# Twelve weight loads moved from SyncE's DMA queue to ScalarE's, in a pooled-attention and spatial-gating kernel

## The chip, the core and the metric

The kernel runs on one core of a Trainium2 chip. A core has a matrix engine (PE; its weight loads are listed apart as PEld), a vector engine (DVE), a scalar engine (ACT, ScalarE), GpSimd (POOL) and SyncE (SP), which here only starts transfers. Each engine works through its own list of instructions in order, and waits on semaphores where it needs another engine or a transfer (DMA). Transfers started by SP or by ACT are carried by the core's 16 DMA engines.

The metric is the device time of one execution in microseconds. It is read as the median of several executions.

## The reference

For each of 8 batches the reference computes attention with 8 heads of 64 on 576 tokens, where keys and values are averaged over groups of 8 tokens (72 pooled ones), and then a gated layer with weights that all batches share. Cut to what matters:

```python
k_p = k.reshape(B, H, Sp, pool, D).mean(axis=3); v_p = ...      # 576 -> 72
attn = softmax(scale * q @ k_p.T);  x = (attn @ v_p) as [B, S, 512]
h = np.maximum(x @ w_in, 0.0)                # w_in [512, 1024]
u, v = h[..., :512], h[..., 512:]
v_n = (v - mean(v)) / np.sqrt(var(v) + 1e-06)
v_s = np.einsum('ts,bsd->btd', w_spatial, v_n) + b_spatial[None, :, None]
out = (u * v_s) @ w_out                      # w_out [512, 512]
```

The inputs reach the device in double width: two 32-bit words stand for each element of `w_in` and `w_out`, so a block of 128 x 512 weights is a transfer of 512 KB, and the kernel makes of it a high part and a low part (`win_h`, `win_l`, `wout_h`, `wout_l`) in the format of the matrix engine.

## The kernel before, in words

All weights, the keys of a batch and its intermediate tiles live on chip. A stage is a short generator: each piece up to a `yield` is one step. The attention stages of a batch are K and KT (keys: load, pool, transpose), V and W (values), Q0 to Q3 (queries of two heads each), S0 to S3 (scores and softmax), T and Y (transposed probabilities) and A (attention output, tile `xT`). The gated layer's are v (`x @ w_in`, right half, and normalisation), u (left half), s (the product with `w_spatial`) and o (the product with `w_out` and the store). Batch after batch the stages of attention for the next batch run between the matrix products of this one.

The weights are loaded once, during the first batch. `wv0` to `wv3` are the four blocks of the right half of `w_in` (128 rows each, line 191, tile `stw`), `wu0` to `wu3` the four of the left half (128 columns each, line 193, tile `stw`), and `wo0` to `wo3` the four of `w_out` (line 191, tile `st`). Each goes through `load_f64`: its first step starts the transfer; its second has ACT read the block (line 202 makes `x` of the high words, line 205 scales the low words, where it is wanted); then DVE (lines 207 to 221) and POOL (lines 212, 213, 224) put the bits together, ACT or POOL writes the high part (lines 229 or 227), and PE and ACT, or POOL (lines 239, 241), the low part.

The order of every engine's work is written out by hand: the string `FIRST` for the first batch, `STEP` for the middle ones, `LAST` for the last. Each word of a string takes the next step of a stage, and all instructions of that step are appended to their engines' lists in that order. A transfer that is started by SP stands in SP's list; one that is started by another engine stands in that engine's list, at the place of its step. Nothing but the string decides that place. `FIRST` begins

```python
"wo1~ -K^ -K wo1 wo1 wo1 -K wv1 -Q0~^ -K wv1 wo1 -K -Q0 wv1 -K wo1 -K wv3^! wv3 -Q1^ wv1 wv1 -KT~ ..."
```

so the second step of `wv3` follows its first one directly, with no other stage between them.

The tiles `stw` are used once for each block and wait for nobody before they are filled. `st` is taken from a ring of three buffers that keys, values and `w_spatial` use too.

Of the kernel before, what the change touches and what calls it, by code (L numbers as in the profile page):

```python
# [10 lines left out]
U32 = mybir.dt.uint32  # L11
# [71 lines left out]
def f32(ap):  # L83
    return ap.bitcast(F32)
# [3 lines left out]
def pooled_attention_gmlp(ctx: ExitStack, tc: tile.TileContext, q, k, v, w_in, w_sp, b_sp, w_out, out):  # L88
    nc = tc.nc
# [9 lines left out]
    NK = DM // P  # L99
# [65 lines left out]
    def ring(tag, bufs, shape, dt, name, pool=pl):  # L165
        return pool.tile(shape, dt, name=name, tag=tag, bufs=bufs)

    def ps_big():
        return ring("mm", 3, [P, 512], F32, "mm", ps)
# [9 lines left out]
    def load_f64(hi, lo, src, alt, st=None):  # L179

        n = DH
        if st is None:
            st = ring("kv", 3, [P, n, 2], U32, "st")
        if len(src.shape) == 2:  # L190
            nc.sync.dma_start(out=st, in_=src.bitcast(U32).rearrange("p (n w) -> p n w", w=2))
        else:
            nc.sync.dma_start(out=st.rearrange("p (c n) w -> p c (n w)", c=NK), in_=src.bitcast(U32))
        yield
        low, high = st[:, :, 0], st[:, :, 1]
        x = ring("vv", 5, [P, n], F32, "x")

        def as_w(ap):
            return ap if len(src.shape) == 2 else ap.rearrange("p (c n) -> p c n", c=NK)

        xi = x.bitcast(U32)
        nc.scalar.activation(x, high.bitcast(F32), AF.Abs, scale=2.0 ** -112)
        if "~" not in alt:
            scaled = low.bitcast(F32)
            nc.scalar.activation(scaled, low, AF.Copy, scale=2.0 ** -52)
        yield
        nc.vector.tensor_scalar(xi, xi, 3, None, op0=ALU.logical_shift_left)
        if "!" in alt:
            yield

            sign, xw = high.bitcast(I32), x.bitcast(I32)
            nc.gpsimd.tensor_scalar(sign, sign, 0.0, -2.0 ** 31, op0=ALU.is_lt, op1=ALU.mult)
            nc.gpsimd.tensor_tensor(xw, xw, sign, op=ALU.add)
            yield
        else:
            nc.vector.scalar_tensor_tensor(xi, high, 0x80000000, xi, op0=ALU.bitwise_and, op1=ALU.bitwise_or)
        y = ring("ob", 2, [P, n], F32, "y")
        nc.vector.tensor_scalar(y.bitcast(U32), xi, 0xFF800000, None, op0=ALU.bitwise_and)
        z = ring("vv", 5, [P, n], F32R, "z") if "^" in alt else y
        if "~" in alt:  # L220
            nc.vector.scalar_tensor_tensor(z, low, 2.0 ** -52, y, op0=ALU.mult, op1=ALU.mult)
        else:
            yield
            nc.gpsimd.tensor_tensor(z, scaled, y, op=ALU.mult)
        yield
        if "%" in alt:
            nc.gpsimd.tensor_copy(hi, as_w(x))
        else:
            nc.scalar.activation(hi, as_w(x), AF.Copy)
        yield  # L230
        if "^" in alt:
            a = ps_big()
            nc.tensor.matmul(a, lhsT=ident, rhs=x, start=True, stop=False)
            nc.tensor.matmul(a, lhsT=ident_m, rhs=hi, start=False, stop=False)
            nc.tensor.matmul(a, lhsT=ident_p, rhs=z, start=False, stop=True)
            yield
            nc.scalar.activation(lo, as_w(a), AF.Copy)
        else:
            nc.gpsimd.tensor_tensor(as_w(x), as_w(x), f32(hi), op=ALU.subtract)
            yield  # L240
            nc.gpsimd.tensor_tensor(lo, as_w(x), as_w(y), op=ALU.add)
# [3 lines left out]
    def load_w_in(half, c, alt=""):  # L245

        tag, n, i = ("gT", NK, c) if half else (("vn_h", "vn_l")[c // 2], 2, c % 2)
        if tag not in staged:

            staged[tag] = pl.tile([P, n, DH, 2], U32, name="stw", tag=tag)  # L250
        cs = slice(c * P, (c + 1) * P)
        if half:
            return load_f64(win_h[:, c, DH:], win_l[:, c, DH:], w_in[cs, DH:], alt, staged[tag][:, i])
        return load_f64(win_h[:, :, cs], win_l[:, :, cs], w_in[:, cs].rearrange("(c p) n -> p c n", p=P), alt,
                        staged[tag][:, i])

    def load_w_out(c, alt=""):
        return load_f64(wout_h[:, c, :], wout_l[:, c, :], w_out[c * P:(c + 1) * P, :], alt)
# [625 lines left out]
```

## Time and profile before

| | before |
|---|---|
| median of 3 runs (lowest to highest) | 551.75 us (551.69 to 552.06) |
| profiled execution, its own time | 551.63 us |
| span of its profile | 549.8 us |
| PE busy | 534.9 us (97%) |
| DVE, ACT, POOL busy | 340.0, 291.6, 278.4 us (62%, 53%, 51%) |
| DMA engines' mean busy share | 42.0% |
| granted TensorE clock | 1.00 |

The span is what lies between the first and the last recorded event; the remaining 1.83 us of the execution lie around it. The chain that ended last is followed back from the last instruction, at each step to what released it. A row of a timeline gives start, duration, engine, line, operation and tiles, and in brackets how long the engine had been idle before and what ended that. SPq is SP's list: the time in such a row is that of starting a transfer, not that of carrying it.

### The profile page before, as it was taken

The numbers are of one execution on the slowest core, as the hardware profiler recorded it, in microseconds if no ns is written. First come the engines' busy times: TensorE is split into PE (matmuls) and PEld (weight loads), VectorE is DVE, ScalarE is ACT, GpSimd is POOL, SyncE is SP. The second block draws the span as 40 slices with busy tenths as digits, with TensorE's granted clock in tenths as the row PEclk, the third lists the DMA queues.
The fourth block names the chain that finished last, engine by engine and source line by source line (L and its number), as shares of the span: only waits on it lengthen the run. The fifth ranks groups of instructions, "written<-read, shape, count | busy, mean of one in ns | idle before, by whom it ended". The sixth has DMA issues, their size and how long they took to land.

```text
span 549.8 us, 11810 instructions
## 1 busy us (share of the span) xinstructions
PE 534.9 (97%) x4293; PEld 477.8 (87%) x4293; DVE 340.0 (62%) x785; ACT 291.6 (53%) x958; POOL 278.4 (51%) x375
## 2 busy tenths in 40 slices
PE   4799999999999999999999999999999999999997
PEld 4588799988998889988998889988998889989995
DVE  3568989987756377675666477675666576623110
ACT  2598788655545365455465365455465554424321
POOL 3845554951457273574825574574825534303340
PEclk9999999999999999999999999999999999999999
DMA  7877463459314363436616264446615232001102
GB/s 242 248 238 157 109 136 111 111 167 236 72 50 115 85 153 76 124 106 153 160 50 162 74 170 107 121 111 155 157 38 136 97 84 93 13 0 39 38 2 97
DMA packets 123354, 63.11 MB, mean 115 GB/s; under 512 B 84256, under 2 KB 104736, under 8 KB 123296
## 3 DMA queue, kind: packets, MB, share of 16 engines
q1 hardware_dynamic: 123296, 62.35, 42.0%
q8 instruction: 34, 0.56, 0.4%
q14 instruction: 24, 0.20, 0.1%
HBM read 44.92 MB, written 17.40 MB: 113 GB/s over the span
## 4 chain that ended last, share of the span: by engine, by line
PE 89%; POOL 3%; ACT 2%; DMA 2%; issue 1%; DVE 1%; SPq 1%; POOLq 0%; ACTq 0%; DVEq 0%
PE mm L780 19%; PE mm L803 18%; PE mm L761 17%; PE mm L718 16%; PE s_ps L530 4%; PE mm L734 2%; DMA qt<-in_q 2%; PE tp L667 2%; PE tp L670 2%; PE mm L781 2%; PE mm L782 2%; PE tp L669 1%; PE tp L668 1%; PE mm L321 1%; POOL vn_l L728 1%
## 5 line engine op out<-in xcount | busy, mean ns | idle before, releaser
L761 PE MATMUL mm<-xT,win_h 128*128 128x320 f32 (+1 forms) x512 | 103.1, 296 | 0.0
L761 PEld LDWEIGHTS mm<-xT,win_h 128*128 128x128 f32 x512 | 82.2, 188 | 2.4
L794 POOL TENSOR_TENSOR gT<-g,gT 128x256 fp32r<-128x256 f32 x64 | 46.5, 736 | 72.5 <-ACT gT L791 72.4
L803 PE MATMUL mm<-wout_h,gT 128*128 128x512 f32 x256 | 79.8, 393 | 0.0
L718 PE MATMUL mm<-win_h,xT 128*128 128x512 f32 x256 | 79.6, 392 | 0.0
L780 PE MATMUL mm<-wT_h,vn_h 128*128 128x256 f32 (+1 forms) x256 | 77.3, 302 | 0.0
L780 PE MATMUL mm<-wT_h,vn_l 128*128 128x256 f32 (+1 forms) x256 | 75.9, 297 | 0.1
L780 PE MATMUL mm<-wT_l,vn_h 128*128 128x256 f32 (+1 forms) x256 | 75.6, 295 | 0.0
L761 PE MATMUL mm<-xT,win_l 128*128 128x320 f32 (+1 forms) x256 | 75.2, 294 | 0.0
L513 POOL TENSOR_TENSOR e<-e,rs 128x576 f32<-128x576 f32 (+1 forms) x32 | 44.9, 1404 | 52.9 <-DVE rs L511 49.4
L785 DVE TENSOR_TENSOR g<-mm,ru 128x256 f32<-128x256 f32 (+1 forms) x64 | 27.7, 450 | 54.1 <-PE mm L782 52.6
L705 POOL TENSOR_TENSOR rstd<-rstd,neg_half 128x1 f32<-128x1 f32 (+1 forms) x40 | 23.2, 583 | 68.3 <-DVE rstd L703 68.2
L506 ACT ACTIVATE e<-s_ps,mx 128x72 f32<-128x72 f32 x190 | 57.6, 332 | 0.2
L728 POOL TENSOR_TENSOR vn_l<-vv,vn_h 128x512 fp32r<-128x512 f32 x32 | 43.0, 1354 | 28.0 <-ACT vn_h L726 28.0
L803 PEld LDWEIGHTS mm<-wout_h,gT 128*128 128x128 f32 x256 | 47.0, 188 | 9.5
L718 PEld LDWEIGHTS mm<-win_h,xT 128*128 128x128 f32 x256 | 47.1, 188 | 9.4
L791 ACT ACTIVATE gT<-g 128x256 fp32r<-128x256 f32 x64 | 25.8, 413 | 47.0 <-DVE g L785 47.0
L699 DVE BATCH_NORM_STATS2 st<-vv 128x6 f32<-128x512 f32 (+1 forms) x40 | 27.3, 682 | 37.7 <-ACT vv L722 37.6
L803 PE MATMUL mm<-wout_l,gT 128*128 128x512 f32 x128 | 50.5, 395 | 0.0
L718 PE MATMUL mm<-win_l,xT 128*128 128x512 f32 x128 | 50.3, 393 | 0.0
L780 PEld LDWEIGHTS mm<-wT_h,vn_h 128*128 128x128 f32 x256 | 48.2, 188 | 2.0 <-ACT ru L764 0.9
L780 PEld LDWEIGHTS mm<-wT_h,vn_l 128*128 128x128 f32 x256 | 48.3, 189 | 0.8 <-POOL vn_l L728 0.5
(191 smaller groups left out, 1260.4 us busy)
## 6 DMA issues: line engine op xcount, KB each, us to landing
st<-in_k SPq DMA_DIRECT2D x32, 256.0 KB, 4.6
out<-ob SPq DMA_DIRECT2D x32, 256.0 KB, 2.0
qt<-in_q SPq DMA_DIRECT2D x112, 72.0 KB, 3.2
st<-in_v SPq DMA_DIRECT2D x24, 256.0 KB, 4.2
xd<-X SPq DMA_DIRECT2D x24, 256.0 KB, 2.5
pt_l<-xd SPq DMA_DIRECT2D x24, 256.0 KB, 3.7
stw<-in_moe_w_in SPq DMA_DIRECT2D x8, 512.0 KB, 7.0
st<-in_moe_w_out SPq DMA_DIRECT2D x4, 512.0 KB
```

The source lines that it names most:

```text
L506: nc.scalar.activation(em[:, h, :], sv[:, h % 2, h // 2, :], AF.Exp, bias=mx[:, h:h + 1], scale=QK, accum_out=sm[:, h:h + 1])
L513: nc.gpsimd.tensor_tensor(em, em, rs.unsqueeze(2).broadcast_to([P, n, SP]), op=ALU.mult)
L699: nc.vector.bn_stats(st6[:m], vv[:m])
L705: nc.gpsimd.tensor_tensor(rstd[:m], rstd[:m], neg_half[:m], op=ALU.pow)
L718: nc.tensor.matmul(a, lhsT=xT[:, i, o + c * P:o + (c + 1) * P], rhs=w[:, i, DH:], start=(i == 0 and j == 0), stop=(i == NK - 1 and j == 2))
L728: nc.gpsimd.tensor_tensor(t["vn_l"][:, c, :], vv, f32(t["vn_h"][:, c, :]), op=ALU.subtract)
L761: nc.tensor.matmul(a, lhsT=w[:, i, d * P:(d + 1) * P], rhs=xT[:, i, o + ts.start:o + ts.stop], start=(i == 0 and j == 0), stop=(i == NK - ...
L780: nc.tensor.matmul(a, lhsT=x[:, c, ds], rhs=y[:, c, ts], start=(c == 0 and j == 0), stop=False)
L785: nc.vector.tensor_tensor(g, a, t["ru"][:, d, ts], op=ALU.mult)
L791: nc.scalar.activation(dst[:, d, 0, at:at + m], g[:, o:o + m], AF.Copy)
L794: nc.gpsimd.tensor_tensor(dst[:, d, 1, at:at + m], g[:, o:o + m], f32(dst[:, d, 0, at:at + m]), op=ALU.subtract)
L803: nc.tensor.matmul(a, lhsT=src[:, i, x, at:at + m], rhs=w[:, i, :], start=(i == 0 and j == 0), stop=(i == ND - 1 and j == 2))
```

## The change

The two lines of `load_f64` that start the transfer of a weight block name `nc.scalar` instead of `nc.sync`. All twelve transfers are those of before, with the same sizes and tiles, and the strings of the order are untouched.

```diff
         if len(src.shape) == 2:
-            nc.sync.dma_start(out=st, in_=src.bitcast(U32).rearrange("p (n w) -> p n w", w=2))
-        else:
-            nc.sync.dma_start(out=st.rearrange("p (c n) w -> p c (n w)", c=NK), in_=src.bitcast(U32))
+            nc.scalar.dma_start(out=st, in_=src.bitcast(U32).rearrange("p (n w) -> p n w", w=2))
+        else:
+            nc.scalar.dma_start(out=st.rearrange("p (c n) w -> p c (n w)", c=NK), in_=src.bitcast(U32))
         yield
```

The lists of PE, DVE and POOL are the same in both kernels. What moves stands in ACT's and SP's lists. At the start of ACT's list, which holds no transfer before, these are the rows of the change (from the first block, `wo1`, over `wv1` and `wv3` to `wv2`):

```order
L191 DMA st<-in_moe_w_out 128x1024
L202 ACT_TABLE_LOAD
L202 ACTIVATE x<-st 128x512
L229 ACTIVATE wout_h<-x 128x512
L191 DMA stw<-in_moe_w_in 128x1024
L202 ACTIVATE x<-stw 128x512
L205 ACTIVATE stw<-stw 128x512
L362 COPY kp<-mm 128x256
L363 COPY kr<-mm 64x128
L191 DMA stw<-in_moe_w_in 128x1024
L202 ACTIVATE x<-stw 128x512
L205 ACTIVATE stw<-stw 128x512
```

The second and the third transfer (`wv1`, `wv3`) stand directly ahead of the instruction that reads what they bring. In SP's list of before these rows stand at the same stage:

```order
L191 DMA st<-in_moe_w_out 128x1024
L344 DMA st<-in_k 128x1x512 x4
L331 DMA st_r<-in_k 64x1x512
L191 DMA stw<-in_moe_w_in 128x1024
L452 DMA qt<-in_q 128x4x64 x2
L453 DMA qt<-in_q 64x2x64
L191 DMA stw<-in_moe_w_in 128x1024
L452 DMA qt<-in_q 128x4x64 x2
```

Without the three weight rows SP's list begins with the keys, and the queries follow them directly. Further on in ACT's list, still in the first batch, the blocks `wu2` and `wu1` come in between the softmax and the copies of the attention output; these are the rows of the change:

```order
L193 DMA stw<-in_moe_w_in 128x4x256
L638 ACTIVATE pt_rr<-tp 32x64 x2
L506 ACTIVATE e,sm<-s_ps,mx 128x72 x10
L175 ACTIVATE xT<-tp 128x256
L193 DMA stw<-in_moe_w_in 128x4x256
L175 ACTIVATE xT<-tp 128x320 x2
L237 ACTIVATE win_l<-mm 128x512
L202 ACTIVATE x<-stw 128x512
```

Here the first of the two (`wu2`) stands some fifteen instructions ahead of line 202, which reads it.

## The prediction

> **What bounds the kernel now.** I read the page first, for the busy shares and the chain that ended last:
>
> ```profile
> PE 534.9 (97%) x4293; PEld 477.8 (87%) x4293; DVE 340.0 (62%) x785; ACT 291.6 (53%) x958; POOL 278.4 (51%) x375
> PE 89%; POOL 3%; ACT 2%; DMA 2%; issue 1%; DVE 1%; SPq 1%; POOLq 0%; ACTq 0%; DVEq 0%
> ```
>
> PE bounds it. Since the moved transfers all lie in the first batch, the stretches come next (columns: stretch, its length, busy time of PE, PEld, DVE, ACT, POOL, granted clock, DMA share, GB/s):
>
> ```profile
> 0.00:25.00 25.00, 15.23 (x158) 12.62 (x158) 11.69 (x30) 9.01 (x17) 13.60 (x18) 1.00 0.80 240
> 25.00:549.00 524.00, 519.67 (x4136) 465.16 (x4136) 328.35 (x756) 282.57 (x941) 264.83 (x358) 1.00 0.41 109
> ```
>
> From 25 us on PE idles 524.00 - 519.67 = 4.33 us in all. So whatever makes PE late by 25 us goes to the end nearly whole. Ahead of 25 us PE idles 9.8 us, and the chain there runs through other engines (the chain in order of time: start, length, what):
>
> ```profile
> 14.74 0.37 ACT kp L362
> ...
> 15.27 0.56 ACT x L202
> 15.83 0.57 ACT stw L205
> 16.41 0.52 ACT win_h L229
> ...
> 24.87 0.49 PE mm L235
> ```
>
> Between the last two stand POOL and DVE with the same block. The rows "ACT x L202" and "ACT stw L205" are the conversion of block `wv3`. They stand on the chain now, with no gap from line 362 to line 229: nothing on ACT can be added there for free. What ACT did and what it waited for (timeline):
>
> ```profile
> 4.42 0.66 ACT L202 ACTIVATE x<-st 128x512 f32<-128x512 f32 x1 [2.42 <-DMA st<-in_moe_w_out]
> 6.30 0.63 ACT L229 ACTIVATE wout_h<-x 128x512 fp32r<-128x512 f32 x1 [1.22 <-DVE x L216]
> 11.64 0.66 ACT L202 ACTIVATE x<-stw 128x512 f32<-128x512 f32 x1 [4.71 <-DMA stw<-in_moe_w_in]
> 12.21 0.66 ACT L205 ACTIVATE stw<-stw 128x512 f32<-128x512 uint32 x1
> 14.74 0.37 ACT L362 COPY kp<-mm 128x256 f32<-128x256 f32 x1 [1.88 <-PE mm L321]
> 15.17 0.67 ACT L202 ACTIVATE x<-stw 128x512 f32<-128x512 f32 x1
> ```
>
> and when SP started those transfers (timeline):
>
> ```profile
> 0.72 0.40 SPq L191 DMA_DIRECT2D st<-in_moe_w_out  x1
> 1.19 2.62 SPq L344 DMA_DIRECT2D st<-in_k  x4
> 4.62 0.40 SPq L191 DMA_DIRECT2D stw<-in_moe_w_in  x1
> 6.85 0.59 SPq L191 DMA_DIRECT2D stw<-in_moe_w_in  x1
> 15.34 0.53 SPq L393 DMA_DIRECT2D st<-in_v  x1
> ```
>
> `wv3` was started at 6.85 us and was there when ACT came to it at 15.17, 8.3 us later: ACT did not wait for it.
>
> **The price of a block, from start to use.** Before, `wo1` took 4.42 - 0.72 = 3.70 us with nothing ahead of it, `wv1` 11.64 - 4.62 = 7.02 us with keys ahead of it. The value blocks of the same size give 6.7 (transfers: KB each, median us to landing), and two windows of the first batch give the rate that the DMA engines reach when they are full:
>
> ```profile
> st<-in_v SPq DMA_DIRECT2D x4, 512.0 KB, 6.7
> 5.00:10.00 5.00, 3.54 (x16) 3.57 (x17) 2.24 (x4) 0.71 (x2) 2.78 (x2) 1.00 0.94 290
> 20.00:25.00 5.00, 3.78 (x40) 2.64 (x31) 3.08 (x6) 1.81 (x5) 4.38 (x4) 1.00 0.97 307
> ```
>
> Alone, 0.524 MB at 0.29 MB/us are 1.8 us, so of `wo1`'s 3.70 some 1.9 are fixed. In a list of its own a block no longer queues behind SP's transfers, but shares the engines with them: at half of 0.307 MB/us it takes 3.4 us, and 5.3 with the fixed part. I take 5.3 and keep 3.7 and 7.0 as ends. The Trainium skill says why half is likely (page "DMA: Bandwidth & Descriptors", section "Queues, rings and completion order"): SP and ACT own one row of rings each, on the same 16 engines, and an engine goes round between the rows packet by packet. No trace here shows it, since before has one such queue. Were a block served as quickly as `wo1` was, with 3.7 in place of 5.3 in steps 2 and 3, the sum below would be 2.8 + 1.0 = 3.8 us and the time 555.4.
>
> **The change part by part.**
>
> 1. *`wo1`* starts at 0.72 as before, but the keys no longer stand behind it. It lands between 4.42 (as before) and 6.46, when PE got its first keys:
>
> ```profile
> 6.46 1.84 PE L321 MATMUL mm<-st,ident 128*128 128x128 f32 x7 [6.46 <-DMA st<-in_k]
> 12.78 0.66 PE L467 MATMUL tp<-ident,qt 128*128 128x128 f32 x4 [0.51 <-DMA qt<-in_q]
> ```
>
>    I take 5.3, near the early end since its start is as early as that of the first keys. From line 202 to the end of line 229 ACT took 6.30 + 0.63 - 4.42 = 2.51 us, so ACT comes to the next transfer at 7.8 (6.9 to 9.0).
>
> 2. *`wv1`* starts there instead of at 4.62, and ACT sits in the next instruction until it lands: 7.8 + 5.3 = 13.1 (6.9 + 3.7 = 10.6 to 9.0 + 7.0 = 16.0). Lines 202 and 205 take 12.21 + 0.66 - 11.64 = 1.23 us: 14.3 (11.8 to 17.2). The cover is ACT's idle 1.88 us ahead of line 362, where it waits for PE to pool the keys. PE may be there earlier than 14.74: SP starts the keys 1.19 - 0.72 = 0.47 us sooner and PE need not wait 0.51 for the queries, so 13.76 at best. Line 362 then starts at 14.3 (13.8 to 17.2), and line 363 ends 15.27 - 14.74 = 0.53 later: 14.9 (14.3 to 17.8).
>
> 3. *`wv3`* is the step that decides. Its transfer stands behind lines 362 and 363, and its reader directly behind it. It starts at 14.9 and lands at 14.9 + 5.3 = 20.2 (14.3 + 3.7 = 18.0 to 17.8 + 7.0 = 24.8). What shares the engines with it are the value block that SP starts at 15.34, and the ones behind it. Line 202 begins at 20.2 and not at 15.17: 5.0 us late (2.8 to 9.6). Queued behind it on ACT are line 205, line 229 (`win_h`), the copies of `qT` and the exponentials. POOL waits for line 229, DVE stands in line 207 for this `x`, ahead of the last copy of the keys, and PE waits for that copy:
>
> ```profile
> 17.00 1.27 POOL L239 TENSOR_TENSOR x<-x,win_h 128x512 f32<-128x512 f32 x1 [1.61 <-ACT win_h L229]
> 16.19 0.42 DVE L207 TENSOR_SCALAR x<-x 128x512 uint32<-128x512 uint32 x1
> 16.52 0.40 DVE L379 COPY kT<-tp 64x32 f32<-64x32 f32 x2
> 16.75 0.95 PE L530 MATMUL s_ps<-kT,qT 64*64 64x72 f32 x32 [0.15 <-DVE kT L379]
> ```
>
>    All of them move by the same 5.0, and no slack is to be seen: POOL had waited 1.61 us for line 229, PE 0.15 for line 379. Late next is everything behind PE's line 235 at 24.87, from where PE has work without a gap.
>
> 4. *The nine later blocks* cost ACT their starting time, and that of SP falls away. By line (ns, minimum, median, maximum) SP took
>
> ```profile
> L191 SPq DMA_DIRECT2D st<-in_moe_w_out x4: 347/376/442, 0.7 to 88.7; - x4
> L191 SPq DMA_DIRECT2D stw<-in_moe_w_in x4: 399/593/687, 4.6 to 22.6; - x4
> L193 SPq DMA_DIRECT2D stw<-in_moe_w_in x4: 503/588/1186, 21.9 to 44.8; - x4
> ```
>
>    I take the same for ACT. It counts where ACT is on the chain:
>
> ```profile
> 37.21 0.21 ACT pt_rr L638
> 37.67 3.14 ACT e L506 x20
> 82.86 0.67 ACT x L202
> ```
>
>    `wu2` starts directly ahead of line 638 at 37.21 and `wo0` just ahead of line 202 at 82.86: 0.59 + 0.38 = 1.0 us. The others stand ahead of an instruction that waits anyway (`wv2` ahead of line 500, which idled 1.85 us for DVE), or behind one that PE needs: nothing. Ends: nothing at all, if these are hidden too, and 0.59 (`wv0`) + 1.19 + 0.59 (`wu1`) + 0.38 = 2.75, if each is paid and `wu2` at its longest.
>
> ```profile
> 19.34 0.68 ACT L500 ACTIVATE e<-e 128x576 f32<-128x576 f32 x1 [1.85 <-DVE e L498]
> 42.02 0.77 ACT L202 ACTIVATE x<-stw 128x512 f32<-128x512 f32 x1
> ```
>
>    Their landing is covered: from `wu2`'s start to its line 202 there are 42.02 - 37.21 = 4.8 us of ACT's own work and two starting times, 6.0 us against 5.3; at 7.0 us it would cost 1.0.
>
> 5. *SP* loses twelve starts. The 0.47 us at the keys are in step 2; later SP waits for buffers, so I count nothing. The Trainium skill (page "Perfetto Trace Analysis", section "DMA Optimizations") has the rule that spreading transfers over issuing engines may help where an engine's issuing is the bottleneck. SP's rows from 0.72 on are dense, so by that rule there would be a gain; it is the rival below.
>
> Sum: 5.0 + 1.0 = 6.0 us. Against the profiled execution's own time, 551.63 (its span of 549.8 and 1.83 around it; 0.12 below the median 551.75), that is **557.6 us**, 1.1% slower.
>
> **The rivals.**
>
> *All early blocks at their late ends.* `wo1` shares fully with the keys, `wv1` and `wv3` take 7.0 each: 9.6 us at step 3, and 1.0: 562.2. For it: the 7.0 and 6.7 above. Against: those were measured behind a full queue, which ACT's list doesn't have.
>
> *Given back later.* The shift eats the 4.33 us that PE idles after 25 us: 557.6 - 4.3 = 553.3. Against: these gaps are waits for engines that are late themselves.
>
> *SP's freed queue wins: faster.* The keys come 0.47 us sooner, PE's 0.51 for the queries goes, and the early starts ahead of keys and queries (0.40 and 0.59) no longer hold SP up: 0.47 + 0.51 + 0.40 + 0.59 = 1.97 us, 549.7. For it: PE's first work waits for keys at 6.46. It decides only if `wv3` makes line 202 less than 1.97 us late, so if it lands by 17.1; started at 14.3 that is 2.8 us, less than the shortest price of 3.7.
>
> *The change doesn't do what it says.* If ACT started transfers ahead of instructions that still wait, `wv3` would be on its way by 8 us and nothing would change: 551.6. Against: it stands behind line 363 in the list, and no row shows an engine's list out of order.
>
> **How the numbers follow.** My forecast has 0.62, the late ends 0.20, the shift given back 0.08, the faster case 0.05, the unchanged one 0.05. The bounds of the forecast alone are 551.63 + 2.8 = 554.4 and 551.63 + 9.6 + 2.75 + 1.0 = 565.0; the upper one needs all ends at once. With the case given back and most of the late one, the range is 553.0 to 563.5. About 0.2% (1.1 us) is what can be told from no change here: faster 0.05, same 0.05, slower 0.90.
>
> **What would show it.** In the changed profile line 202 should wait for `stw<-in_moe_w_in` twice, the second time some 5 us around 20 us; POOL's line 239 on `win_h` should start at 22 and PE's line 235 near 30. From there to the end the span should be as long as before, within 1 us or so. I am wrong if line 202 for `wv3` does not wait, if PE's line 235 comes at 25 to 27 us, or if the time is lost behind 30 us.

## The result, and the profile after

The changed kernel takes 555.61 us (median of 4 runs, 555.12 to 556.42), the kernel before in the same series 551.72. The ratio is 1.0074, with a 95% interval of 1.0061 to 1.0087: 3.9 us or 0.7% slower. The forecast was 557.6 us. The profiled execution took 555.23 us, 1.83 around a span of 553.4, so it lies 3.6 us above that of before and at the low side of its runs.

The page of the changed kernel, busy shares and the chain that ended last:

```profile
PE 536.4 (97%) x4293; PEld 479.5 (87%) x4293; DVE 340.4 (62%) x785; ACT 291.6 (53%) x958; POOL 278.7 (50%) x375
PE 90%; DMA 3%; ACT 2%; POOL 2%; DVE 1%; issue 1%; SPq 0%; POOLq 0%; ACTq 0%; DVEq 0%
```

ACT's busy time is the same to the tenth (291.6), since starting a transfer is not counted as busy. The page hardly shows the change; DMA on the chain rose from 2% to 3%. The timeline of ACT shows it (rows with ACTq are the starts):

```profile
6.34 0.63 ACT L229 ACTIVATE wout_h<-x 128x512 fp32r<-128x512 f32 x1 [1.22 <-DVE x L216]
8.13 0.34 ACTq L191 DMA_DIRECT2D stw<-in_moe_w_in  x1
12.33 0.67 ACT L202 ACTIVATE x<-stw 128x512 f32<-128x512 f32 x1 [5.36 <-DMA stw<-in_moe_w_in]
12.91 0.67 ACT L205 ACTIVATE stw<-stw 128x512 f32<-128x512 uint32 x1
12.91 0.33 ACTq L191 DMA_DIRECT2D stw<-in_moe_w_in  x1
13.47 0.35 ACT L362 COPY kp<-mm 128x256 f32<-128x256 f32 x1
18.21 0.66 ACT L202 ACTIVATE x<-stw 128x512 f32<-128x512 f32 x1 [4.22 <-DMA stw<-in_moe_w_in]
```

Line 202 now waits for `stw` twice. The first wait, for `wv1`, is 5.36 us instead of 4.71. The second, for `wv3`, is new: 4.22 us, and line 202 begins at 18.21 instead of 15.17, 3.04 us late. The chain of waits runs through both transfers:

```profile
2.76 5.34 DMA st<-in_k
8.13 4.18 DMA stw<-in_moe_w_in
12.33 0.58 ACT x L202
12.91 5.27 DMA stw<-in_moe_w_in
18.21 0.67 ACT x L202
18.90 0.43 DVE x L207
19.33 0.10 DVE kT L379
19.47 1.49 PE s_ps L530 x32
...
58.14 5.51 PE mm L718 x24
...
535.35 13.76 PE mm L803 x60
```

The chain of before has the last two of these rows as well:

```profile
55.15 5.51 PE mm L718 x24
...
532.33 13.76 PE mm L803 x60
```

So the shift is 58.14 - 55.15 = 2.99 us at the first group of line 718 and 535.35 - 532.33 = 3.02 us at the last group of line 803. What was lost by 19 us is carried through 480 us unchanged; on balance nothing is added on the way and nothing given back. The chain puts the second start down to the end of line 202 at 12.91; PE had pooled the keys 0.04 us before that, at 12.87, so this profile alone can't tell which of the two the start followed. Who waited for `wv3` is seen at POOL and PE:

```profile
20.02 1.27 POOL L239 TENSOR_TENSOR x<-x,win_h 128x512 f32<-128x512 f32 x1 [3.95 <-ACT win_h L229]
19.47 1.46 PE L530 MATMUL s_ps<-kT,qT 64*64 64x72 f32 x32 [3.16 <-DVE kT L379]
```

PE's wait for the last copy of the keys went from 0.15 to 3.16 us, POOL's for line 229 from 1.61 to 3.95.

The rest of the difference in span, 3.7 - 3.0 = 0.7 us, stands behind the last copy. The waits of SP's queue in the last microseconds (idle us, count, longest), in the changed kernel:

```profile
SPq L880 <- DMA out<-ob: 2.2, 1, 2.2
```

Before it was 1.5 us. The DMA queues of the changed kernel between 549 and 554 us (packets, MB, share of the engines' time; q14 carries the fetches of instructions) show what else was moved then:

```profile
q1 hardware_dynamic: 144, 0.26, 13.8%
q14 instruction: 1, 0.01, 0.8%
```

Beside the last output a fetch of instructions ran. The page counts 25 of them in the changed kernel, 24 before, where none falls into the last output.

### The profile page after: what moved, and what is told of

Its sections match the earlier page's. It is cut to its first block, busy times and chain, and to the rows that moved or that the text cites. A ratio compares the mean times of both kernels' runs of the same rounds, so it can differ in the third digit from the quotient of the medians.

```text
span 553.4 us, 11813 instructions
## 1 busy us (share of the span) xinstructions
PE 536.4 (97%) x4293; PEld 479.5 (87%) x4293; DVE 340.4 (62%) x785; ACT 291.6 (53%) x958; POOL 278.7 (50%) x375
## 4 chain that ended last, share of the span: by engine, by line
PE 90%; DMA 3%; ACT 2%; POOL 2%; DVE 1%; issue 1%; SPq 0%; POOLq 0%; ACTq 0%; DVEq 0%
PE mm L780 19%; PE mm L803 18%; PE mm L761 17%; PE mm L718 15%; PE s_ps L530 4%; PE mm L734 2%; PE mm L321 2%; PE tp L667 2%; DMA stw<-in_moe_w_in 2%; PE tp L670 2%; PE mm L781 2%; PE mm L782 2%; PE tp L669 1%; PE tp L668 1%; DMA st<-in_k 1%
```

## The experiments

The theory is step 3 of the prediction: the start of `wv3` stands on ACT behind a wait (line 362, for PE's pooled keys), its reader right behind it, so the whole way from start to landing is exposed, and nothing else counts. The rivals: the other eleven blocks share in the loss (starts on ACT, `wv1` that comes late, sharing of the DMA engines), or it is the granted clock, which fell in the changed kernel (below).

The first experiments choose a queue for each block; with this edit and a list of the blocks that ACT's queue loads:

```diff
+ON_ACT = 'wv3'.split()
...
-    def load_f64(hi, lo, src, alt, st=None):
+    def load_f64(hi, lo, src, alt, st=None, dma=nc.sync):
...
-            nc.sync.dma_start(out=st, in_=src.bitcast(U32).rearrange("p (n w) -> p n w", w=2))
+            dma.dma_start(out=st, in_=src.bitcast(U32).rearrange("p (n w) -> p n w", w=2))
...
-    staged = {}
+    staged, queue = {}, lambda kind, c: nc.scalar if f"{kind}{c}" in ON_ACT else nc.sync
```

Each call of `load_f64` passes `queue(...)` of its block. All results in one table; "line 202" is the start of line 202 for `wv3`, "line 235" PE's first instruction of line 235 (a weight load), "last copy" the start of the last line 807, each in the profiled execution (before: 15.17, 24.87, 546.16).

| kernel | on ACT | us (before) | ratio, 95% interval | line 202 | line 235 | last copy |
|---|---|---|---|---|---|---|
| the change | all 12 | 555.61 (551.72) | 1.0074 [1.0061, 1.0087] | 18.21 | 27.87 | 549.18 |
| e_wv3_only | `wv3` | 556.43 (551.62) | 1.0087 [1.0073, 1.0101] | 19.22 | 28.89 | 550.07 |
| e_not_wv3 | all but `wv3` | 553.62 (551.62) | 1.0036 [1.0023, 1.0049] | 15.43 | 26.61 | 547.87 |
| e_nine_late | nine later ones | 552.46 (551.62) | 1.0014 [1.0005, 1.0022] | 14.80 | 24.53 | 547.06 |
| e_eight_late | these without `wv2` | 552.06 (551.62) | 1.0012 [1.0003, 1.0020] | 15.30 | 25.36 | 546.47 |
| e_hoist | all, `wv3` started early | 553.08 (551.62) | 1.0023 [1.0014, 1.0032] | 14.34 | 25.04 | 546.32 |
| e_warm | all, extra products on PE | 555.98 (551.62) | 1.0081 [1.0068, 1.0095] | 19.89 | 29.54 | 550.65 |
| e_hoist_warm | both of these | 553.12 (551.62) | 1.0026 [1.0015, 1.0036] | 13.78 | 23.97 | 545.56 |
| e_all_but_wo2 | all but `wo2` | 556.03 (551.51) | 1.0070 [1.0053, 1.0086] | 19.27 | 29.34 | 550.82 |
| e_three_hoist_warm | `wo1`, `wv1`, `wv3` early, extra products | 551.16 (551.62) | 0.9987 [0.9978, 0.9996] | 14.61 | 24.80 | 545.85 |
| e_wo1_only | `wo1` | 551.14 (551.51) | 0.9989 [0.9981, 0.9998] | 14.73 | 24.45 | 545.73 |
| e_wo1_wv3_hoist | `wo1`, `wv3` early | 551.00 (551.51) | 0.9990 [0.9981, 0.9998] | 14.63 | 24.35 | 545.77 |

### Only wv3 on ACT

> Only block wv3 is started by ACT, the other eleven by SP as before. Theory A (one transfer that stands directly ahead of its reader in ACT's list makes ACT wait, and that shifts the rest): ACT comes to the start at some 14.5 us, the block lands some 5.3 us later, line 202 begins near 19.7 and not at 15.2, and the time is 4.0 to 4.7 us above before, so at least as much as with all twelve moved (3.9). Rival B (the cost is spread over the twelve starts on ACT, or comes from the second queue as such): one block costs well under half of 3.9 us, 0.3 to 1.5 us.

Measured +4.8 us, just above the 4.0 to 4.7 of theory A and somewhat more than the whole change. The timeline of ACT:

```profile
14.04 0.37 ACT L362 COPY kp<-mm 128x256 f32<-128x256 f32 x1 [1.41 <-PE mm L321]
14.05 0.41 ACTq L191 DMA_DIRECT2D stw<-in_moe_w_in  x1
14.31 0.26 ACT L363 COPY kr<-mm 64x128 f32<-64x128 f32 x1
19.22 0.66 ACT L202 ACTIVATE x<-stw 128x512 f32<-128x512 f32 x1 [4.66 <-DMA stw<-in_moe_w_in]
```

The transfer starts as soon as line 362 has stopped waiting for PE, and line 202 comes 5.17 us later. One block of twelve is enough for the loss. Line 202 is 1.01 us later than in the profile of the change (19.22 against 18.21), since PE pools the keys later here, and that goes with the larger loss.

### All but wv3 on ACT

```diff
-ON_ACT = 'wv3'.split()
+ON_ACT = 'wo1 wv1 wv2 wu0 wv0 wu2 wu1 wu3 wo3 wo0 wo2'.split()
```

> All blocks but wv3 are started by ACT. Theory A: line 202 finds wv3 landed, so nothing of the 3.9 us is left; the keys are pooled sooner, so the time is 0 to 1.2 us below before. Rival B: eleven twelfths of 3.9 us, some 3.5 us above before. Rival C (wv1, the other block that stands directly ahead of its reader, has a share of its own): 1 to 2 us above before.

Measured +2.0 us, the upper end of rival C: with the block that loses 4.8 by itself taken out, the change still loses. The timeline of ACT, and the rows of PE behind it:

```profile
8.62 0.34 ACTq L191 DMA_DIRECT2D stw<-in_moe_w_in  x1
13.89 0.67 ACT L202 ACTIVATE x<-stw 128x512 f32<-128x512 f32 x1 [7.06 <-DMA stw<-in_moe_w_in]
15.43 0.69 ACT L202 ACTIVATE x<-stw 128x512 f32<-128x512 f32 x1
```

```profile
16.86 0.66 PE L467 MATMUL tp<-ident,qt 128*128 128x128 f32 x4 [0.80 <-DVE qT L474]
18.07 1.01 PE L530 MATMUL s_ps<-kT,qT 64*64 64x72 f32 x32 [0.35 <-DVE kT L379]
```

Now `wv1` is late by itself: started at 8.62, used at 13.89 instead of 11.64. `wv3` (at 15.43) waits for nothing, but DVE has `wv1`'s conversion to do ahead of a copy that PE waits for (0.80 us), and PE's line 530 comes at 18.07 instead of 16.75. That is not the whole of the 2.0. The granted clock is 0.50 from 19 to 25 us here, and PE's products of line 321 ahead of line 235 take 3.67 us; the third row is that of before, at 1.00:

```profile
24.27 1.30 POOL L224 TENSOR_TENSOR z<-stw,y 128x512 fp32r<-128x512 f32 x1 [0.54 <-DVE y L218]
22.23 3.67 PE L321 MATMUL mm<-st,ident 128*128 128x128 f32 x16
```

```profile
20.24 2.05 PE L321 MATMUL mm<-st,ident 128*128 128x128 f32 x16
```

POOL has `wv3` ready for line 235 at 25.57, and PE comes there only at 26.61. So 1.0 of the 1.7 us that line 235 is late goes with the half clock. What `wv1` costs by itself was not measured, since it was never moved alone. The losses don't add up: without `wv3` the change costs 2.0, `wv3` alone 4.8, all together 3.9; a late `wv3` may cover what `wv1` does, but that is not shown. The theory holds for the change, but "nothing else counts" is too strong.

### The nine later blocks alone, and without wv2

```diff
-ON_ACT = 'wv3'.split()
+ON_ACT = 'wv2 wu0 wv0 wu2 wu1 wu3 wo3 wo0 wo2'.split()
```

> wo1, wv1 and wv3 are started by SP as before, the nine later blocks by ACT. Step 4 of the prediction: 1.0 us above before (0 to 2.75). Theory A with what the trace of the change shows (a start on ACT's queue runs while ACT still works on the instruction ahead of it): no change, within 0.4 us. If the second queue lengthens the end of the program, the last event is some 0.6 us later behind the last copy of line 807 than in before.

Measured +0.8 us, near the 1.0 of step 4. But the place is another one. Line 235 is early (24.53); PE then waits for a value block, by the waits of PE and the timeline of SP in that execution:

```profile
PE mm L321 <- DMA st_r<-in_v: 1.3, 1, 1.3
```

```profile
18.51 1.28 SPq L344 DMA_DIRECT2D st<-in_k  x2
22.82 1.92 SPq L331 DMA_DIRECT2D st_r<-in_v  x2
```

Before, the transfer of line 331 was started at 20.62. Here it is 2.2 us later. SP's start waits, as the trace is read here, for an earlier transfer (16.26) to complete, and that one now shares the engines with `wv2` (512 KB, started by ACT at 16.27), which before stood behind it in SP's own list. That reading was tested by putting `wv2` back:

```diff
-ON_ACT = 'wv2 wu0 wv0 wu2 wu1 wu3 wo3 wo0 wo2'.split()
+ON_ACT = 'wu0 wv0 wu2 wu1 wu3 wo3 wo0 wo2'.split()
```

> As the kernel with the nine later blocks on ACT (0.8 us above before), but wv2 is started by SP again, so eight are on ACT. If the loss there is PE's wait of 1.3 us for the rest of the values, whose transfer SP starts late since an earlier one shares the engines with wv2: that wait is gone and the time is within 0.4 us of before. If it is the starts on ACT: 0.7 us above before, since eight of nine remain.

PE's wait of 1.3 us is gone. The list of PE's waits between 12 and 60 us has one wait for a transfer left:

```profile
PE tp L467 <- DMA qt<-in_q: 0.7, 1, 0.7
```

It ends at 12.91 us, ahead of the first start on ACT (19.98), and before has the same wait with 0.51, so the moved blocks have no part in it. The time is 0.4 us above before, between the two cases, and 0.4 lower than with `wv2`, and the intervals of the two overlap. So the trace shows a wait that comes and goes with `wv2`; that it makes the 0.8 us of the nine, the times don't decide. It isn't the starts on ACT that step 4 counted (in the trace with all nine): line 638 is 1.03 us late (38.24 instead of 37.21), line 718 by the same 1.03 (56.18), the last copy by 0.90, and the start ahead of line 638 ran at 35.74 while ACT worked on line 202 (35.37 to 36.05).

### All on ACT, but wv3 started right behind wv1

```diff
-    "wo1~ -K^ -K wo1 wo1 wo1 -K wv1 -Q0~^ -K wv1 wo1 -K -Q0 wv1 -K wo1 -K wv3^! wv3 -Q1^ wv1 wv1 -KT~ -Q0 -KT "
+    "wo1~ -K^ -K wo1 wo1 wo1 -K wv1 wv3^! -Q0~^ -K wv1 wo1 -K -Q0 wv1 -K wo1 -K wv3 -Q1^ wv1 wv1 -KT~ -Q0 -KT "
```

The word `wv3^!` is the step that starts the transfer of `wv3`; it now stands ahead of ACT's wait for `wv1`. The list of blocks is that of the change.

> All twelve blocks are started by ACT as in the change, but the first step of wv3 stands directly behind that of wv1 in the order, so its start comes ahead of the wait for wv1. Theory A: both start near 8.1 us and share the engines, wv3 lands by 13 to 15 us, line 202 waits for it no more than 1 us, and the time is between 1.2 us below and 0.3 us above before. Rival B: as the change, 3.9 us above before, since the same twelve starts are on ACT.

Measured +1.5 us: moving one start takes away more than half of the loss. Neither case has it so: theory A allowed 0.3 us at most, rival B 3.9. ACT in its trace:

```profile
8.12 1.37 ACTq L191 DMA_DIRECT2D stw<-in_moe_w_in  x2
12.47 0.67 ACT L202 ACTIVATE x<-stw 128x512 f32<-128x512 f32 x1 [5.68 <-DMA stw<-in_moe_w_in]
14.34 0.68 ACT L202 ACTIVATE x<-stw 128x512 f32<-128x512 f32 x1 [0.21 <-DMA stw<-in_moe_w_in]
```

Both transfers are started in one go from 8.12 on, and line 202 for `wv3` is 0.83 us earlier than before the change. In the profiled execution (552.36 us) line 235 and the last copy are within 0.2 us of before, and most of what is left is the longer end. Why the median is not below 553 the one profile doesn't say. Its PE came to half the granted clock in this stretch (length, busy PE, PEld, DVE, ACT, POOL, clock, DMA share, GB/s):

```profile
13.00:16.00 3.00, 1.49 (x13) 0.92 (x10) 2.75 (x7) 2.79 (x7) 1.07 (x1) 1.00 0.69 156
17.00:23.00 6.00, 5.59 (x85) 4.81 (x84) 3.97 (x7) 1.33 (x3) 5.20 (x5) 0.50 0.89 258
```

### Is it the clock?

In the changed kernel the granted clock fell too, from 16 us on, while PE waited, and it was still 0.50 when PE worked again:

```profile
16.00:20.00 4.00, 0.84 (x13) 0.65 (x16) 0.71 (x3) 1.79 (x4) 0.08 (x1) 0.50 0.96 249
20.00:25.00 5.00, 4.58 (x79) 3.81 (x73) 3.03 (x5) 1.22 (x3) 4.81 (x4) 0.50 0.96 342
26.00:27.00 1.00, 1.00 (x10) 1.00 (x10) 1.00 (x2) 1.00 (x2) 0.49 (x1) 0.99 0.54 177
```

To tell the clock from the wait, products of the identity that nothing reads were put into PE's list (a stage that the kernel has for it, `warm`, line 274; each `wd` is four products), at three places of the change:

```diff
-    ... wv1 wv1 -KT~ -Q0 -KT "
+    ... wv1 wv1 wd0 -KT~ -Q0 wd2 -KT "
...
-    ... -V^ -Q3^ -KT -S0 ...
+    ... -V^ -Q3^ -KT wd4 wd6 -S0 ...
```

> The change, and with it 16 products of the identity with itself that nothing reads, put into PE's list at three places between 13 and 19 us, so that PE does not stand still there. Theory A (ACT's wait alone sets the loss; POOL's chain behind it ends at 27.8 us, where PE's line 235 begins at 28.0 in the change): the granted clock stays at 1.00 and the time is that of the change within 0.3 us, 3.5 to 4.0 us above before. Rival D (the granted clock, which is 0.50 from 16 to 26 us in the change, has a share of the loss of its own): 0.7 us or more below the change.

Measured +4.4 us, no gain over the change and more than the 3.5 to 4.0 of theory A, at a clock of 1.00 throughout:

```profile
0.00:25.00 25.00, 16.23 (x173) 14.83 (x174) 9.23 (x25) 7.35 (x13) 9.50 (x15) 1.00 0.82 230
```

The lower clock is thus not what the change cost. The trace of the change says the same, by POOL's last piece of `wv3`:

```profile
26.51 1.30 POOL L224 TENSOR_TENSOR z<-stw,y 128x512 fp32r<-128x512 f32 x1 [0.54 <-DVE y L218]
```

It ends at 27.81, and PE begins line 235 at 27.87, so a faster PE could have begun it no more than 0.1 us earlier. From line 202 for `wv3` to line 235 are 9.66 us in the change at half clock, 9.65 here at full clock and 9.70 before. It is otherwise where `wv3` is not late: there PE at half clock comes later than POOL, by 1.0 us without `wv3` on ACT (above) and by 0.8 in e_hoist (25.04 against 24.25).

The chain of e_warm shows what line 202 for `wv3` follows:

```profile
13.51 1.08 PE mm L321 x16
14.62 0.01 ACT kp L362
14.63 5.24 DMA stw<-in_moe_w_in
19.89 0.35 ACT x L202
```

PE ended pooling the keys at 14.59, here 1.7 us later than in the profile of the change (12.87); line 362's wait ends, the transfer starts, 5.24 us later it is there. The price is that of the change (5.27); the start differs from execution to execution with the keys.

The same products with `wv3` started early (the edit of the order above, with `wd0` and `wd2` alone):

> As the kernel with the start of wv3 directly behind that of wv1 (1.3 us above before), and 8 products of the identity with itself that nothing reads, at two places between 13 and 16 us. There POOL was done with wv3 at 24.2 us, but PE came to line 235 only at 25.3, at a granted clock of 0.50. Rival D here: the clock stays at 1.00, line 235 begins near 24.2, and the time is 1.0 us below that kernel, 0.3 us above to 0.8 us below before. Without a share of the clock: as that kernel, 1.3 us above before.

The kernel without them is at +1.5 us in the table, where the text has 1.3. The median (553.12) is that of the kernel without them; the 1.0 us expected did not come. In its profiled execution, 551.84 us, the clock was 1.00 and line 235 came at 23.97, 1.07 us sooner than in e_hoist, but its other runs go up to 553.84. What makes the runs of these two kernels spread by two microseconds stays open.

### The longer end

```diff
-ON_ACT = 'wo1 wv1 wv3 wv2 wu0 wv0 wu2 wu1 wu3 wo3 wo0 wo2'.split()
+ON_ACT = 'wo1 wv1 wv3 wv2 wu0 wv0 wu2 wu1 wu3 wo3 wo0'.split()
```

> The change, but its last block, wo2, is started by SP again; ACT's list is one start shorter. In the change an instruction fetch (queue q14, a 25th one) runs while the last output is written, and the program ends 4.26 us behind the last copy of line 807 instead of 3.59. If that fetch is what lengthens the end: with the shorter list it comes later or not at all, the end takes 3.6 us again, and the time is 0.6 us below the change, 3.0 to 3.3 us above before; the last copy of line 807 is as late as in the change (3.0 us). If the end is longer for another reason (the second queue as such): as the change, 3.9 us above before.

With one block back on SP there are 24 fetches, and the last wait of SP is as before:

```profile
SPq L880 <- DMA out<-ob: 1.5, 1, 1.5
```

From the last copy to the end are 3.60 us, against 4.26 in the change and 3.59 before. In all kernels of the table with 25 fetches (the change, e_hoist, e_warm, e_hoist_warm) it was 4.2 to 4.5, in all others 3.6 to 3.8. In these four the last fetch falls 1.4 to 1.8 us behind the last copy, in the other nine profiles none falls there. So the longer end goes with the fetch in every profile. That the fetch causes it is not shown: these four are also the ones with all twelve starts on ACT, and the fetch was never changed alone. The expected time was missed: 0.6 less than the change was to come, and 556.03 was measured. Line 202 explains the profiled execution: PE ended pooling at 13.91, `wv3` started at 13.94 and landed 5.3 us later, and the last copy is 4.66 late instead of 3.02. The variation of that start hides 0.6 us.

### What is to be had

> wo1, wv1 and wv3 on ACT with the start of wv3 directly behind that of wv1, the nine later blocks on SP as before, and 8 products of the identity that nothing reads as above. If the keys' earlier start and the earlier conversion of wv3 are kept to the end: 0.3 to 1.1 us below before. If the freed time is lost again between 25 and 55 us: within 0.3 us of before.

This kernel has the order of e_hoist with `wd0` and `wd2`, and `ON_ACT = 'wo1 wv1 wv3'.split()`. It is the first that is faster than the kernel before, by 0.13%, and next to e_hoist_warm it says that the nine later blocks on ACT cost some 2 us in the medians (553.12 against 551.16). The two profiles don't show these 2 us: they differ by 0.6 (551.84 against 551.24), 0.9 at the end (4.48 against 3.61 us behind the last copy) and 0.3 the other way ahead of it. Where the rest arises stays open, as the 0.8 of these nine did.

> wo1 alone is started by ACT, at the start of the program where ACT has nothing else; the other eleven by SP as before. The rival of the prediction on the other side, taken alone: the keys start 0.47 us sooner and no block stands ahead of its reader in ACT's list, so 0.4 to 1.0 us below before. If the keys lose as much by sharing the engines with wo1: within 0.3 us of before.

`ON_ACT = 'wo1'.split()`, the order of before. PE's first keys in its trace:

```profile
6.02 5.80 PE L321 MATMUL mm<-st,ident 128*128 128x128 f32 x32 [6.02 <-DMA st<-in_k]
```

They come at 6.02 instead of 6.46, and line 202 for `wv3` (14.73), line 235 (24.45) and the last copy (545.73) are each 0.4 us early. It fits the 0.47 us of SP's first start, and the medians differ by as much (551.14 against 551.51). The profile alone doesn't show that it comes from there: in the one with the nine later blocks on ACT, whose early blocks start as before, lines 202 and 235 are as early (14.80 and 24.53), with the first keys at 6.80. The keys' arrival itself does go with the start: 6.46 to 6.80 us in the four profiles with `wo1` on SP, 5.77 to 6.45 in the nine with it on ACT.

> wo1 and wv3 on ACT, the start of wv3 ahead of the instruction that waits for wv1; wv1 and the nine later blocks on SP as before. wv1 starts at 4.2 us and lands by 12, wv3 by 14 to 15. If the conversion of wv3 is early then: 0.4 to 1.2 us below before; if wv3 lands behind 15.2 us: at or above before.

`ON_ACT = 'wo1 wv3'.split()` with the order of e_hoist: 0.39 us early at the last copy, no better than `wo1` alone. A `wv3` that starts early enough on ACT costs nothing here and brings nothing. All three beat both kernels, that of before by 0.4 to 0.5 us, with intervals that stay below 1, though by less than the 1.1 us that the prediction set as the bound of what can be told. The simplest is `wo1` alone.

## Why the prediction was right, and where not

The direction, the place and the mechanism were right, and the time lies in the range and in the likeliest case's bounds (554.4 to 565.0). The size was 6.0 against 3.9 us. That it came so near is in part luck: in the profile step 3 was too high by 2.0 us and step 4 by 1.0, and 0.7 us at the end, which the prediction didn't have, made up for some of it. The 555.4 that it named for blocks served as quickly as `wo1` is nearest to the result, and by luck too: that price was 3.7, and 5.27 was measured.

- *What bounds the kernel.* Right. PE has no slack behind 25 us: the shift is 3.00 us at line 235 and 3.02 at the last copy. The rival that gives 4.3 us back falls.
- *Step 1.* `wo1` was used at 4.46, at the early end; 5.3 was too much. From its start it took 3.74 us, as before (3.70), though the keys no longer stood behind it.
- *Step 2.* Near in the sum, since two errors offset each other. ACT ended line 229 at 6.97 and not at 7.8, but `wv1` started only at 8.13: by the chain above the start itself waited for a transfer of the keys. It landed 4.18 us later, between the ends of 3.7 and 7.0. Line 205 ended at 13.58; 14.3 was forecast.
- *Step 3* is the term that was mis-sized: 5.0 forecast, 3.04 measured. Its price was right: 5.27 us from start to landing against 5.3, and 5.15 to 5.30 in three more profiles. The start was wrong: 12.91 and not 14.9. The prediction put it behind the end of line 363. What it is behind is only the *waits* ahead of it in the list. In the change the last two were over at 12.87 (PE's pooling, for line 362) and 12.91 (line 202), and the start went out at 12.91 while ACT still worked on line 205, ahead of lines 362 and 363 at 13.47 and 13.72. In three more profiles PE's pooling alone is last, and the start follows it by 0.03 to 0.04 us. Of the 2.0 us between forecast and start 13.98 - 12.91 = 1.07 come from that; in the other 0.92 `wv1` and the keys came sooner than steps 1 and 2 had them. With the start of e_warm's execution, 14.63, nearly the forecast's, line 202 was 4.72 late, nearly its 5.0. That the price came right is not proof of its parts, 1.9 us fixed and half the engines: from 12.9 to 18.2 us the packets of ACT's queue took 39.0% of the engines' time and those of SP's 57.3%, so the queues did share, but not by halves. `wo1` had 47.5% against 23.5% between 0.7 and 4.5 us, beside keys that SP was still starting up to 3.4 us. The Trainium skill (page "DMA: Bandwidth & Descriptors", section "Queues, rings and completion order") has each engine go round between the queues' rows packet by packet; the trace agrees that both queues were served at once.
- *Step 4.* Wrong for the change: 1.0 forecast, nothing measured (2.99 us late at 58 us, 3.02 at the end). The starts of 0.33 us run beside ACT's work, like that at 12.91 beside line 205. What the nine cost when alone, 0.8 us, is by its trace another mechanism (a value block held back behind `wv2`), one that the prediction didn't have and that the times don't settle.
- *Step 5.* It counted nothing for SP beyond step 2. The 0.47 us there are borne out by e_wo1_only (0.4 us in the medians), and with the keys' early arrival they may be part of why step 3's start came sooner. The rival that SP's freed queue wins names an effect that exists, but it is wrong in the change, since `wv3` is later than its limit of 1.97 us; with `wo1` alone it is worth 0.4 us, not 1.97.
- *Not seen at all.* 0.7 us at the end, with a fetch of instructions during the last output. 3.0 + 0.7 = 3.7 is the profile's difference in span; without it the miss would have been larger.

The late rival (7.0 us a block) falls by the 5.27 and 4.18. The rival that the change doesn't do what it says is nearest to what was missed in step 3: starts do go out ahead of work that is queued, but not ahead of a wait.

## What to carry to other kernels

A transfer that ACT starts here goes out only when ACT's earlier waits are over. Where a computing engine starts transfers, ask which wait stands ahead of the start and how far its reader stands behind it, for what lies between them is all that covers the way of the transfer, 5.3 us here. Moving the start is worth more than choosing the queue: `wv3` on ACT costs 4.8 us behind the wait and nothing ahead of it. And of a set of transfers moved together, try the ones that stand first in the crowded list, for every kernel here that gained has `wo1` on ACT, and `wo1` alone gained nearly as much.

## What the runs showed of the hardware

- A start on ACT runs beside ACT's own instruction (0.33 us at 12.91, beside line 205 of 0.67), and goes out ahead of instructions whose waits are already over.
- A start can itself wait for an earlier transfer that shares no tile with it, as the chains are read: in the change `wv1`, from 6.97 to 8.13 us, goes out 0.02 us behind the landing of a transfer of the keys, and the same in three more profiles (8.12, 8.55, 8.62). Why is not shown.
- The granted clock went to 0.50 in the changed kernel about 16 us and stayed there to 26 us, though PE was busy 4.58 of the 5 us from 20 on; in e_hoist it fell as well, with PE busy for 1.49 of the 3 us ahead. The Trainium skill (page "TensorE: Matmul & The Clock Gate", section "Part 1: The HAM clock gate (the "warmup" mystery)") gives a busy window of about 3.4 us, which runs free of the kernel, for the way back to full rate; the trace agrees on the half rate, but PE worked some 6 us at it, nearly two such windows, before the clock returned in both kernels.
- A fetch of instructions during the last output goes with 0.6 us more between the last copy and the end (4.2 to 4.5 us in four profiles, 3.6 to 3.8 in nine).
